# Attention and a GELU layer in one kernel: the last chunk's output stores joined to one per block, and two sums of chunk 2 moved behind the group sums

## The chip, the cores and the metric

The kernel runs on one core of a Trainium2 chip. The core has five engines that work side by side: TensorE (PE in the profile; its weight loads are PEld), VectorE (DVE), ScalarE (ACT), GpSimd (POOL) and SyncE (SP), which issues DMA transfers and computes nothing. ScalarE can issue transfers as well. Sixteen DMA engines move the data between the chip's memory and the core. The metric is the device time of one execution in microseconds (us).

## What is computed

Eight batches, eight heads, 576 positions, 64 columns per head. Linear attention, then a dense layer, an exact GELU and a second dense layer:

```python
q_s = softmax(q, axis=-1)          # per position
k_s = softmax(k, axis=2)           # over the positions
kv  = einsum('bhsd,bhse->bhde', k_s, v)
att = einsum('bhsd,bhde->bhse', q_s, kv)
x   = att.transpose(0, 2, 1, 3).reshape(4608, 512)
h   = x @ w_in                      # 512 x 2048
out = gelu(h) @ w_out               # 2048 x 512, 4608 rows of float32
```

(The two softmax lines stand for the reference's max, exp, sum and division.)

## The kernel before

**Chunks.** The 4608 rows of the output are 8 batches of 576 positions. Chunks 0 to 7 take the first 512 positions of one batch each (M = 512). The 64 positions that each batch has left (R = 64) are collected from all eight batches into a ninth chunk of 512 rows, chunk 8, which comes last. Inside chunk 8, block column j of half `half` holds two batches, 2 * (2 * half + j) and the one after it: partitions 0 to 63 belong to the first, 64 to 127 to the second.

**The order** in which each engine works is written out by hand: every engine and every queue runs its instructions in the order in which the code issues them, and waits on semaphores where it needs what another has made.

**Products with seven factors.** For chunks 2 to 8 the first dense layer is done by a scheme with 7 half-size products in place of 8 (`h_waves`), and so is the second layer of chunks 1 to 8 (`y_phase`, and `y_last` for chunk 8). Sums and differences of operands and of partial results, made on VectorE, take the place of the eighth product.

`h_waves` takes its output in four groups q = 0 to 3, in two waves: groups 0 and 1, then 2 and 3. `mm(m, q, ...)` issues product m for the groups named. Products accumulate in banks of the accumulator memory, kept in `held`: "A" (written by products 1, 6, 7, 4; in the profile qa), "B" (5 and 3; qb) and "C" (a copy of A, then product 2; qc). `seed(q)` copies A to C, `p5_copy(q)` copies B aside to `r`, `e_sum(q)` adds A to B (DVE qb L428), `r_sum(q)` adds A to `r` (DVE r L428). Product 7 writes into A again and so can't begin for a group before that group's `e_sum` has read A; product 4 can't before `r_sum`. `gelu(kind, ...)` on ScalarE takes a finished bank into `g`. `h_waves` is called with `mid` only for chunk 2; then the wave order is a little different, and the seeds of groups 2 and 3 are copied on VectorE.

`s_parts(c, p0, n, which)` makes the sums of `g` that the second layer needs, on VectorE: 0 makes `s5` (L393), 3 and 4 make the two halves of `s12` (L402), 2 two differences in place (L404, L405). `s12` is read by products 1 and 2 of the second layer, `s5` by product 5. In every chunk from 2 on, the add number 3 for rows 0 to 3 stands in `h_waves` ahead of `mm(6, 2, 3)` and the two group sums `e_sum(2)`, `e_sum(3)`; number 4 stands right behind those.

**The last chunk's output.** `y_last` computes chunk 8's rows in 128x256 blocks: two block columns j, and for each two halves of rows (`ysb[0]`, `ysb[1]`) and two halves of columns (c0 = 0 or 256), eight blocks in all. Each block's sum ends on VectorE (L428) or, for three of them, ScalarE (L769, L774). Then `store` sends the block out, with one transfer for each of the two batches: 64 partitions, 64 rows of 256 floats. Fourteen of these sixteen transfers are issued by SyncE; of the last two blocks one transfer each is issued by ScalarE (`both`). The tensor `dst` is `out` seen as [u, s, j, n]: batch parity, position, batch pair, column.

A transfer issued by SyncE or ScalarE carries one of eight semaphores in turn, and waits for the transfer that had the same one before it. The program ends when every transfer has landed.

The stores of the other chunks (`y_store`, L635) move 512 KB each: 128 partitions, one row of 4 KB each.

Of the kernel before, what the change touches and what calls it, by code (L numbers as in the profile page):

```python
# [16 lines left out]
def kernel(  # L17
# [16 lines left out]
    nc = tc.nc  # L34
    B, H, S, D = q.shape
# [3 lines left out]
    M = 128 * J  # L39
    R = S - M  # L40
# [25 lines left out]
    def bank(i, name="ps", shape=(128, 512)):  # L66
        return psum.tile(list(shape), FP32, tag=f"k{i}", name=name)
# [21 lines left out]
    HN = DM // 2  # L89
# [282 lines left out]
    def h_begin(c):  # L372
        st[c]["g"] = moe_sb.tile([128, NDF, M], BF16, tag="g", name="g", bufs=1)
# [53 lines left out]
    def tt(out, in0, in1, op=ALU.add, eng=nc.vector):  # L427
        eng.tensor_tensor(out=out, in0=in0, in1=in1, op=op)  # L428
# [33 lines left out]
    def h_waves(c, mid):  # L462

        h_begin(c)
        g, xT = st[c]["g"], st[c]["xT"]
        t1, t2, t3, t4 = (quad["t"][:, i] for i in range(4))
        mov = {1: xT[:, 0:2, 0:HT], 2: xT[:, 2:4, 0:HT], 3: xT[:, 2:4, HT:M], 4: t4, 5: t1, 6: t2, 7: t3}
        plain_w = {1: (0, 0), 2: (2, 0), 4: (2, HK)}  # L470
        sum_w = {3: 3, 5: 0, 6: 1, 7: 2}
        lo, hi = slice(0, HT), slice(HT, M)
        bank_of = {
            "A": ("bb", "x0", "x3", "ba"), "B": ("kv0", "kv1", "x1", "x2"), "C": ("x1", "x2", "kv0", "kv1"),
        }
        held = {}

        def take(kind, q):
            held[kind, q] = bank(roles[bank_of[kind][q]], "q" + kind.lower(), (128, 2, HT))

        def mm(m, *qs):
            for q in qs:
                kind = {5: "B", 3: "B", 2: "C"}.get(m, "A")
                if m in (1, 5):
                    take(kind, q)
                for u in range(2):
                    for k in range(2):
                        if m in plain_w:
                            k0, t0 = plain_w[m]
                            t = 2 * q + t0 + u  # L490
                            w = wi_bf[:, k0 + k, t * 128:(t + 1) * 128]
                        else:
                            t = 2 * (q % 2) + u
                            w = quad["s"][q // 2][:, sum_w[m], k, t * 128:(t + 1) * 128]
                        nc.tensor.matmul(  # L495
                            held[kind, q][:, u], w, mov[m][:, k],
                            start=(m in (1, 5) and u == 0 and k == 0), stop=(k == 1),
                            skip_group_check=True,
                        )

        def seed(q, eng=nc.scalar.copy):
            take("C", q)
            eng(out=held["C", q], in_=held["A", q])  # L503

        def p5_copy(q, eng):
            held["r", q] = quad["r"][:, q]
            eng(out=held["r", q], in_=held["B", q])

        def e_sum(q):
            tt(held["B", q], held["A", q], held["r", q])  # L510

        def r_sum(q):
            tt(held["r", q], held["A", q], held["r", q])

        def gelu(kind, *qs):
            up, half = {"C": (1, lo), "B": (1, hi), "A": (0, lo), "r": (0, hi)}[kind]
            for q in qs:
                t = 2 * q + (0 if up else HK)
                nc.scalar.activation(out=g[:, t:t + 2, half], in_=held[kind, q], func=AF.Gelu)  # L519

        vcopy, scopy = nc.vector.tensor_copy, nc.scalar.copy
        mm(1, 0, 1)
        seed(0)
        if mid:
            seed(1)
            mm(1, 2, 3)
            mm(2, 0, 1)
            gelu("C", 0, 1)
            mm(5, 0, 1)
        else:  # L530
            mm(5, 0, 1)
            seed(1)
        p5_copy(0, scopy)
        p5_copy(1, scopy)
        mm(6, 0, 1)
        x_sums(c, (3, 4) if mid else (3,))
        e_sum(0)
        e_sum(1)
        if not mid:
            x_sums(c, (4,))  # L540
        if mid:
            mid()
            mm(5, 2, 3)
            p5_copy(2, scopy)
            p5_copy(3, scopy)
        else:
            mm(2, 0, 1)
            gelu("C", 0, 1)
        mm(7, 0, 1)
        r_sum(0)  # L550
        r_sum(1)
        mm(3, 0, 1)
        if not mid:
            for q in (2, 3):
                mm(5, q)
                mm(1, q)
        mm(4, 0, 1)
        if mid:
            gelu("B", 0)
            seed(2, vcopy)  # L560
            gelu("B", 1)
            seed(3, vcopy)
            gelu("r", 0, 1)
        else:
            gelu("r", 0)
            gelu("B", 0, 1)
            gelu("r", 1)
            seed(2)
            seed(3)
        gelu("A", 0, 1)  # L570
        if not mid:
            p5_copy(2, vcopy)
            p5_copy(3, vcopy)
        s_parts(c, 0, 4, (3,))
        mm(6, 2, 3)
        e_sum(2)
        e_sum(3)
        s_parts(c, 0, 4, (4,))
        mm(2, 2, 3)
        gelu("C", 2, 3)  # L580
        mm(7, 2, 3)
        r_sum(2)
        r_sum(3)
        gelu("r", 2, 3)
        mm(3, 2, 3)
        mm(4, 2, 3)
        gelu("A", 2, 3)
        gelu("B", 2, 3)
        s_parts(c, 0, 4, (0,))
        s_parts(c, 0, 4, (2,))  # L590
        s_parts(c, 4, 4, (0,))
        s_parts(c, 4, 4, (3,))
        s_parts(c, 4, 4, (4,))
        turn_roles()
# [125 lines left out]
    def y_last(c):  # L720

        act, wgt = y_operands(c)
        names = (("x0", "yd"), ("x2", "yx"), ("x1", "ye"), ("ba", "ya"), ("bb", "yb"),
                 ("x3", "yd"), ("kv0", "ye"), ("kv1", "yb"))
        bd, bx, be, ba, bb, bd1, be1, bb1 = (bank(roles[r], n) for r, n in names)
        banks = [(bd, be, bb, ba), (bd1, be1, bb1, None)]
        ysb = [moe_sb.tile([128, 2, DM], FP32, tag="y_sb", name="y_sb", bufs=2) for i in range(2)]
        dst = out.rearrange("(j u s) n -> u s j n", j=J, u=2)  # L730

        def store(half, j, c0, engs):
            for u, eng in enumerate(engs):
                eng.dma_start(
                    out=dst[u, M:S, 2 * half + j, c0:c0 + HN],
                    in_=ysb[half][u * R:(u + 1) * R, j, c0:c0 + HN],
                )

        halves = [[(bank(roles["x2"], "ya") if ps is None else ps)[:, 0:HN] for ps in banks[j]] for j in range(2)]

        def mm(j, m, ps, first):
            for k in range(HK):
                nc.tensor.matmul(  # L743
                    ps, act[m][:, k, j * 128:(j + 1) * 128], wgt[m][:, k, :],
                    start=(first and k == 0), stop=(k == HK - 1), skip_group_check=True,
                )

        def parts(j):
            f = zeros32[:, j * HN:(j + 1) * HN]
            return (f, ysb[0][:, j, 0:HN], ysb[0][:, j, HN:DM], ysb[1][:, j, 0:HN], ysb[1][:, j, HN:DM])  # L750

        one = (nc.sync, nc.sync)
        both = (nc.scalar, nc.sync)
        for j in range(2):
            bd, be, bb, ba = halves[j]
            f, c11, c12, c21, c22 = parts(j)
            mm(j, 4, bd, True)
            nc.scalar.copy(out=f, in_=bd)
            if j == 0:
                mm(j, 3, bx[:, 0:HN], True)  # L760
                nc.scalar.copy(out=c12, in_=bx[:, 0:HN])
            mm(j, 5, be, True)
            tt(f, f, be, ALU.subtract)
            mm(j, 1, ba, True)
            tt(c22, f, ba)
            if j == 0:
                tt(c12, c12, be)
            mm(j, 2, bd, False)
            nc.scalar.copy(out=c21, in_=bd)  # L769
            store(1, j, 0, one)  # L770
            tt(c22, c22, c21, ALU.subtract)
            if j:
                mm(j, 3, be, False)
                nc.scalar.copy(out=c12, in_=be)  # L774
            store(0, j, HN, one)
            tt(c22, c22, c12)
        for j in range(2):
            bd, be, bb, ba = halves[j]
            f, c11, c12, c21, c22 = parts(j)
            mm(j, 6, bb, True)  # L780
            tt(c22, c22, bb)
            store(1, j, HN, both if j else one)
            mm(j, 7, ba, False)
            tt(c11, f, ba)
            store(0, j, 0, both if j else one)

    wi_cols = [256, 256, 512, 512, 512]
    wi_parts = [1, 1, 4, 2, 2]
# [337 lines left out]
```

## Time and profile before

| | |
|---|---|
| median of 3 runs | 259.1 us (258.95 to 259.1) |
| profiled execution | 259.09 us, of which span 257.3 us (first to last instruction) |
| TensorE clock granted over the span | 0.994 |
| TensorE, VectorE, ScalarE, GpSimd busy | 248.6, 208.2, 188.9, 67.6 us |
| sum of the last block done | 252.17 us |
| last store issued | 254.34 us |

In a profile line such as `L428 DVE TENSOR_TENSOR y_sb<-zeros,ya 128x256 f32` the line of the code comes first, then engine, operation, the tile written and those read, and the shape; `x14` counts the instructions of a group. In a timeline the first two numbers are start and length in us; in the chain of waits each line is a piece of the chain of work that ended last. `ACTq` and `SPq` are the sequencers that issue transfers. In the table by windows each engine shows its busy time; the last columns are the granted clock, the mean busy share of the 16 DMA engines and the GB/s that they moved. A DMA queue's line shows packets, MB and its share of the 16 engines' time. A line of DMA issues shows how many, their size and the median time from issue to landing.

The page's view of the span in 40 slices shows where each engine and the DMAs are busy; TensorE is full until the last two slices:

```profile
PE   7899999999999999999999999999999999999991
...
DMA  7999999993449905980598059805910420040024
```

### The profile page before, as it was taken

Reading aid. Unit: us, or ns where it says so; the run is one execution under the profiler, and the core shown is the slowest. Engines: PE = TensorE matmul, PEld = TensorE weight load, DVE = VectorE, ACT = ScalarE, POOL = GpSimd, SP = SyncE. Lnnn points to the kernel's source line nnn. Section 1 sums busy time; section 2 is a strip of 40 time slices with the busy share of each in tenths; the row PEclk is TensorE's granted clock in tenths of the full one; section 3 lists DMA queues with packets and bytes.
Section 4 is the critical chain, followed back from the end, with each engine's and each line's share of the span. In section 5 each row is a group of like instructions: output and inputs, shape, how many; then the busy total and the mean of one; then the engine's idle time right before and its main releaser. Section 6 shows DMA issues by size and latency. Waiting matters only on the chain.

```text
span 257.3 us, 6512 instructions
## 1 busy us (share of the span) xinstructions
PE 248.6 (97%) x2670; PEld 195.1 (76%) x2670; DVE 208.2 (81%) x364; ACT 188.9 (73%) x320; POOL 67.6 (26%) x65
## 2 busy tenths in 40 slices
PE   7899999999999999999999999999999999999991
PEld 3444444448887888888888888888888888888880
DVE  1878796998978979896989798979897989398951
ACT  4876887799978895899589958995896686068610
POOL 1530024001645067006700670067002700040000
PEclk9999999999999999999999999999999999999997
DMA  7999999993449905980598059805910420040024
GB/s 240 399 384 425 402 405 400 397 414 133 84 153 346 263 17 143 315 326 1 137 305 338 3 131 333 316 0 132 250 33 0 130 117 3 0 160 8 1 64 102
DMA packets 43166, 50.23 MB, mean 195 GB/s; under 512 B 20224, under 2 KB 30464, under 8 KB 42880
## 3 DMA queue, kind: packets, MB, share of 16 engines
q1 hardware_dynamic: 42736, 49.39, 56.9%
q10 hardware_dynamic: 400, 0.43, 0.7%
q8 instruction: 21, 0.34, 0.5%
q14 instruction: 9, 0.07, 0.1%
HBM read 36.70 MB, written 9.44 MB: 179 GB/s over the span
## 4 chain that ended last, share of the span: by engine, by line
PE 91%; DMA 4%; DVE 1%; ACT 1%; issue 0%; ACTq 0%; POOL 0%; DVEq 0%
PE qa L495 18%; PE ps L377 11%; PE ya L673 10%; PE yd L673 10%; PE qb L495 9%; PE ye L673 5%; PE ps L616 5%; PE yb L673 5%; PE qc L495 4%; PE yx L673 4%; PE kv L225 2%; DMA f<-in_v_dram 2%; DMA touch<-in_moe_w_in_dram 2%; PE ps L343 2%; PE ya L743 1%; PE yd L743 1%
## 5 line engine op out<-in xcount | busy, mean ns | idle before, releaser
L495 PEld LDWEIGHTS <-quad_s 128*128 128x128 bf16 x448 | 43.8, 98 | 6.1 <-issue 1.0
L673 PEld LDWEIGHTS <-g 128*128 128x128 bf16 x448 | 43.3, 98 | 5.8 <-issue 0.4
L269 POOL TENSOR_TENSOR e<-e,recq 128x2048 bf16<-128x2048 bf16 (+1 forms) x9 | 27.4, 3047 | 73.4 <-DVE recq L264 40.5
L495 PEld LDWEIGHTS <-wi_bf 128*128 128x128 bf16 x336 | 32.8, 98 | 4.0
L673 PEld LDWEIGHTS <-s 128*128 128x128 bf16 x336 | 32.9, 98 | 3.8
L495 PE MATMUL qa<-quad_t,quad_s 128*128 128x256 bf16 x224 | 29.5, 272 | 0.2
L377 PE MATMUL ps<-xT,wi_bf 128*128 128x512 bf16 x128 | 28.3, 379 | 0.0
L428 POOL TENSOR_TENSOR y_sb<-y_sb 128x512 f32<-128x512 f32 x14 | 19.4, 1389 | 24.2 <-DVE y_sb L428 21.3
L263 DVE TENSOR_REDUCE qsum<-e 128x16 f32<-128x1024 bf16 (+1 forms) x12 | 20.9, 1746 | 4.9 <-ACT e L173 4.8
L377 PEld LDWEIGHTS <-wi_bf 128*128 128x128 bf16 x128 | 12.2, 98 | 15.4 <-DVE wi_bf L814 0.9
L503 ACT COPY qc<-qa 128x512 f32<-128x512 f32 x26 | 13.9, 577 | 12.0 <-PE qa L495 11.5
L519 ACT ACTIVATE g<-r 128x512 bf16<-128x512 f32 x28 | 17.3, 630 | 7.3 <-DVE r L428 7.3
L428 DVE TENSOR_TENSOR qb<-qa,r 128x512 f32<-128x512 f32 x28 | 18.1, 693 | 5.5 <-ACT g L519 3.1
L383 ACT ACTIVATE g<-ps 128x512 bf16<-128x512 f32 x32 | 17.8, 600 | 6.1 <-PE ps L377 5.8
L173 ACT ACTIVATE e<-f 128x512 bf16<-128x512 f32 (+1 forms) x42 | 20.5, 556 | 2.1 <-DMA f<-in_q_dram 2.1
L519 ACT ACTIVATE g<-qc 128x512 bf16<-128x512 f32 x28 | 15.2, 594 | 7.1 <-PE qc L495 7.1
L402 DVE TENSOR_TENSOR s<-g 128x1024 bf16<-128x1024 bf16 x28 | 18.5, 682 | 0.2 <-ACT g L519 0.2
L190 POOL CAST v_aug<-f 128x576 bf16<-128x576 f32 x26 | 17.6, 709 | 4.2 <-DMA f<-in_v_dram 3.9
L428 DVE TENSOR_TENSOR r<-qa,r 128x512 f32<-128x512 f32 x28 | 18.0, 682 | 0.7 <-PE qa L495 0.4
L178 ACT ACTIVATE ek<-f 128x2304 bf16<-128x2304 f32 (+1 forms) x10 | 17.2, 1734 | 0.5 <-DMA f<-in_k_dram 0.5
L519 ACT ACTIVATE g<-qb 128x512 bf16<-128x512 f32 x28 | 15.1, 595 | 0.7 <-PE qb L495 0.7
L495 PE MATMUL qb<-quad_t,quad_s 128*128 128x256 bf16 x112 | 15.5, 273 | 0.0
(100 smaller groups left out, 466.8 us busy)
## 6 DMA issues: line engine op xcount, KB each, us to landing
out_dram<-y_sb SPq DMA_DIRECT2D x16, 512.0 KB, 3.4
f<-in_k_dram SPq DMA_DIRECT2D x6, 1152.0 KB, 9.6
f<-in_v_dram SPq DMA_DIRECT2D x6, 1152.0 KB, 11.6
f<-in_q_dram SPq DMA_DIRECT2D x6, 1024.0 KB, 7.9
w<-in_moe_w_in_dram SPq DMA_DIRECT2D x6, 512.0 KB, 9.3
f<-in_v_dram SPq DMA_DIRECT2D x8, 288.0 KB, 6.3
f<-in_q_dram SPq DMA_DIRECT2D x4, 512.0 KB, 9.0
w<-in_moe_w_out_dram SPq DMA_DIRECT2D x2, 1024.0 KB, 11.9
```

The costliest lines, as they stand in the source:

```text
L173: nc.scalar.activation(out=dst[:, i], in_=src[:, u], func=AF.Exp)
L178: nc.scalar.activation(out=ek[b % 2][:, i:i + n], in_=st[b]["kf"][:, i:i + n].rearrange("p x (n d) -> p x n d", n=NS), func=AF.Exp,)
L190: eng.tensor_copy(out=o, in_=i)
L263: nc.vector.reduce_sum(out=qsum, in_=st[b]["eq"][:, :, i * w:(i + 1) * w, :], axis=AX.X)
L269: eng.tensor_tensor(out=e, in0=e, in1=st[b]["recq"].unsqueeze(3).to_broadcast([128, J, w, D]), op=ALU.mult,)
L377: nc.tensor.matmul(ps, wi_bf[:, dm, t * 128:(t + 1) * 128], st[c]["xT"][:, dm, :], start=(dm == 0), stop=(dm == NDM - 1),)
L383: nc.scalar.activation(out=st[c]["g"][:, t, :], in_=ps, func=AF.Gelu)
L402: tt(out=s12[:, a, half], in0=g[:, a, half], in1=g[:, b, hi], op=ALU.add)
L428: eng.tensor_tensor(out=out, in0=in0, in1=in1, op=op)
L495: nc.tensor.matmul(held[kind, q][:, u], w, mov[m][:, k], start=(m in (1, 5) and u == 0 and k == 0), stop=(k == 1), skip_group_check=True,)
L519: nc.scalar.activation(out=g[:, t:t + 2, half], in_=held[kind, q], func=AF.Gelu)
L673: nc.tensor.matmul(ps[:, j * HN:(j + 1) * HN], act[m][:, k, j * 128:(j + 1) * 128], wgt[m][:, k, :], start=(first and k == 0 and j == 0), ...
```

## The change

Two edits.

1. In `y_last`, `store` issues one transfer per block instead of two. Its source is the block's 128 partitions, its target `dst[:, M:S, ...]`, with the two batches as the outermost dimension: 2 x 64 rows of 256 floats, the two batches being 576 rows of `out` apart. Eight transfers are left. Six are issued by SyncE; those of the two blocks `store(0, 1, HN)` and `store(0, 1, 0)` by ScalarE. None of the eight shares its semaphore with another of them any more.
2. In `h_waves` with `mid` (chunk 2 alone), the add number 3 of `s12` for rows 0 to 3 moves from ahead of `mm(6, 2, 3)` and the group sums to behind the group sums, where number 4 was; number 4 moves to behind `s5`'s first add. The other chunks keep their order. The instructions are the same ones.

```diff
@@ h_waves
-        s_parts(c, 0, 4, (3,))
+        if not mid:
+            s_parts(c, 0, 4, (3,))
         mm(6, 2, 3)
         e_sum(2)
         e_sum(3)
-        s_parts(c, 0, 4, (4,))
+        s_parts(c, 0, 4, (3,) if mid else (4,))
         mm(2, 2, 3)
...
         s_parts(c, 0, 4, (0,))
+        if mid:
+            s_parts(c, 0, 4, (4,))
         s_parts(c, 0, 4, (2,))
@@ y_last
-        def store(half, j, c0, engs):
-            for u, eng in enumerate(engs):
-                eng.dma_start(
-                    out=dst[u, M:S, 2 * half + j, c0:c0 + HN],
-                    in_=ysb[half][u * R:(u + 1) * R, j, c0:c0 + HN],
-                )
+        def store(half, j, c0, eng=nc.sync):
+            eng.dma_start(
+                out=dst[:, M:S, 2 * half + j, c0:c0 + HN],
+                in_=ysb[half][:, j, c0:c0 + HN],
+            )
...
-        one = (nc.sync, nc.sync)
-        both = (nc.scalar, nc.sync)
...
-            store(1, j, 0, one)
+            store(1, j, 0)
...
-            store(0, j, HN, one)
+            store(0, j, HN, nc.scalar if j else nc.sync)
...
-            store(1, j, HN, both if j else one)
+            store(1, j, HN)
...
-            store(0, j, 0, both if j else one)
+            store(0, j, 0, nc.scalar if j else nc.sync)
```

## The prediction

> **What bounds the kernel now.** I read the page first, then the timeline of the last 15 us, the DMA issues, the busy time by windows, and the chain of waits around chunk 2's second pair of groups.
>
> ```profile
> span 257.3 us, 6512 instructions
> ...
> PE 248.6 (97%) x2670; PEld 195.1 (76%) x2670; DVE 208.2 (81%) x364; ACT 188.9 (73%) x320; POOL 67.6 (26%) x65
> ...
> PE 91%; DMA 4%; DVE 1%; ACT 1%; issue 0%; ACTq 0%; POOL 0%; DVEq 0%
> ```
>
> TensorE is 91% of the chain: a change of order pays only where TensorE waits. After its last product the kernel has only stores left, and there the end is set by who issues and moves them:
>
> ```profile
> 251.33 1.37 ACTq L734 DMA_DIRECT2D out_dram<-y_sb  x2
> 251.75 0.42 DVE L428 TENSOR_TENSOR y_sb<-zeros,ya 128x256 f32<-128x256 f32 x1 [0.45 <-PE ya L743]
> ```
> ```profile
> 254.34 0.55 SPq L734 DMA_DIRECT2D out_dram<-y_sb  x1
> ```
>
> The last sum is done at 251.75 + 0.42 = 252.17. SyncE is still issuing: its last store goes out at 254.34, since 14 issues of 0.47 to 1.35 us each stand in one queue. That store lands 2.0 us later (next fence), at 256.34, and the span ends 0.96 later. So about 4.2 us lie between the last sum and the last landing, 2.2 of them SyncE's queue.
>
> ```profile
> out_dram<-y_sb SPq DMA_DIRECT2D x14, 64.0 KB, 2.0
> ...
> f<-in_k_dram ACTq DMA_DIRECT2D x1, 288.0 KB, 3.1
> ...
> out_dram<-y_sb ACTq DMA_DIRECT2D x2, 64.0 KB, 2.0
> touch<-in_v_dram ACTq DMA_DIRECT2D x1, 0.1 KB, 4.1
> ```
> ```profile
> q10 hardware_dynamic: 400, 0.43, 0.7%
> ```
>
> q10 is ScalarE's queue, and its packets can be counted out. It carries one load of 128 rows, three of 16 rows (touch, of v, w_in and w_out) and two stores of 64 rows: 128 + 48 + 128 = 304 rows, at one packet a row. The other 96 are 16 for each of the six transfers, one closing packet per DMA engine. So every transfer was cut into 16 pieces, even the one of 16 rows of 8 bytes: the cut goes by rows, not by bytes. In all of them the first dimension on both sides is 128, 64 or 16.
>
> **The stores.** Removed: 16 issues, each of 64 rows of 1 KB. Added: 8 issues, each of 128 rows of 1 KB, six on SyncE and two on ScalarE (the last two blocks of output columns that finish on it). The bytes stay at 1 MB, 1024 packets. What is new is the shape of the target: [2 batches][64 rows][256], against 128 partitions at the source. No profiled transfer has a first dimension below 16, so the number of engines that share such a transfer is unknown, and has to be bounded from both sides: 16, as in all rows above, or 2, one for each index of the first dimension. I take 2. The cut seen above goes by rows, and a target whose first dimension has two entries 576 rows apart can be cut along it only once; to get 16 pieces the cut would have to go through two dimensions together, which no transfer here shows.
>
> The Trainium skill says the same in "DMA: Bandwidth & Descriptors", "Why a DMA increments its semaphore by 16 and not by 1": the number of engines is the largest up to 16 that divides the slowest dimension, other than 1, of both sides. By that rule each new store uses 2 engines and the result is the forecast. Its section "Rules for kernel authors" also says the opposite of halves: one transfer of 128 partitions rather than two of disjoint halves; that advice alone would give rival A. No run here shows either yet.
>
> Pace of one engine on 1 KB packets, from two ends:
>
> ```profile
> core 0: us, PE busy (x) PEld busy (x) DVE busy (x) ACT busy (x) POOL busy (x), PEclk, DMA share, GB/s
> 3.50:5.50 2.00, 2.00 (x4) 0.77 (x3) 0.00 (x0) 1.09 (x3) 0.00 (x0) 1.00 1.08 378
> ...
> 229.20:231.00 1.80, 1.80 (x19) 1.62 (x17) 1.69 (x4) 1.22 (x4) 0.00 (x0) 1.00 0.99 403
> 252.00:254.00 2.00, 0.00 (x0) 0.00 (x0) 0.17 (x1) 0.00 (x0) 0.00 (x0) 1.00 0.67 162
> ```
>
> From 3.5 to 5.5 the first loads of q run, rows of 1 KB over 128 partitions: 378 / (1.08 x 16) = 21.9 GB/s for a busy engine, 46.8 ns a packet. From 252 to 254 the old stores run, over 64 partitions each: 162 / (0.67 x 16) = 15.1, or 67.8 ns. From 229.2 to 231 the stores of chunk 7 run, rows of 4 KB: 403 / (0.99 x 16) = 25.4, which for 1 KB would be 40.3 ns. So storing is not slower in itself; the 67.8 belongs to sixteen engines crowding on half the partitions. Two engines, one for each half, are nearer to the first window: I take 46.8 and keep 40.3 and 67.8 as ends. (The page named above gives about 27 GiB/s an engine; that would be 35 ns and, as an estimate, 266.4 us.)
>
> With two engines each store puts 64 packets on each, 64 x 46.8 ns = 3.0 us, and I take it that all eight use the same two (else it is rival C). The eight become ready within 7.9 us (first issue 244.28, last sum 252.17) but need 24 us of service, so from the second store on the two engines are never idle, and neither which queue issues a store nor how fast matters. The first issue moves to 243.85 (next part). Fixed cost of a store: 2.0 us less its four packets per engine of 68 ns, 1.73. Last landing: 243.85 + 1.73 + 512 x 0.0468 = 269.54, where it was 256.34. Nothing in the program is queued behind the stores but the closing waits, so no engine's work is held; the old cover, TensorE's products up to 251.7, hides only the first 7 us of it.
>
> **Chunk 2's s12.** VectorE's add of the first half of s12 (L402) stood before the two group sums. The chain there, and TensorE's products:
>
> ```profile
> 80.86 0.64 ACT g L519
> ...
> 81.52 0.69 DVE s L402
> 82.21 0.62 DVE qb L428
> ...
> 82.88 1.19 PE qa L495 x8
> ```
> ```profile
> 80.75 1.19 PE L495 MATMUL qa<-quad_t,quad_s 128*128 128x256 bf16 x8
> 81.78 1.04 PE L495 MATMUL qc<-xT,wi_bf 128*128 128x256 bf16 x8
> 82.88 1.19 PE L495 MATMUL qa<-quad_t,quad_s 128*128 128x256 bf16 x8
> ```
>
> Eight products follow each other in 0.87 us (first start to next group's first start, elsewhere in this chain). Group 82.88 could start at 81.78 + 0.87 = 82.65: 0.23 lost, and inside it 1.19 - 1.04 = 0.15 more while it waits for the second group sum. The last group of this wave takes 1.08 rather than 1.04, 0.04 more. Sum 0.42, say 0.43 with roundings. In the new order a group sum starts when its products are done. For the first pair of groups VectorE started 0.11 after the end of the fourth product (76.71 to 76.82). Here the fourth starts at 80.75 + 3 x 0.11 = 81.08 and takes 0.27 (the page's mean), so the first sum starts at 81.46; the second group's products start at 81.35, held by the seed as before, and its sum at 82.06; with 0.69 each they end at 82.15 and 82.75, ahead of 82.65 and 83.09 when TensorE wants the banks. The add of s12 itself now runs 82.66 to 83.35, when the first r sum's products are just done (83.37). So the stall goes and no new one comes. The other half of s12 (0.69) moves behind s5; VectorE has as many adds in that stretch as before, so those after it keep their times (the last of s12 ended at 88.82, the last in place at 90.15, for which GpSimd waits). The first reader of s12 is the product at 90.94, or 90.51 now: 1.7 us cover it. Without that cover up to 0.69 would come back; with it all 0.43 stay. No DMA is issued by what is moved, and nothing of SyncE's or GpSimd's queue is passed. The 0.15 inside the group at 80.75 is a wait for the seeds, which stays. After 82.88 the chain is TensorE to the end, so I pass 0.43 on to it.
>
> **The sum**, against the profiled execution: 259.09 us, of which the span is 257.30 and 1.79 lies around it; it is within 0.01 of the median, 259.1. New: 269.54 + 0.96 + 1.79 = 272.29, so +13.2 = -0.43 (chunk 2) + 13.6 (tail). With 40.3 ns it is 269.0, with 67.8 ns 283.0.
>
> **Rivals.**
> A. The cut still gives 16 engines (faster). The same formula gives the end 243.85 + 1.73 + (1024 / k) x 0.0468 for k engines, until the last issue decides. With 16, SyncE's queue of 14 is gone, the last store goes out on ScalarE at 251.77 and lands after 2.2 (2.0 and four more packets per engine): 253.97 + 0.96 + 1.79 = 256.7, 2.4 us less. For it: every transfer of the page was cut in 16, and the count of rows, 128, is a multiple of 16. Against: the cut never had to cross a dimension. It decides from k = 5 on: break-even with 256.34 is at 1024 x 0.0468 / 10.76 = 4.5 engines.
> B. Two engines, at the pace of the old stores' packets: 283.0. For it: the same rows of out, in the same direction. Against: the crowding goes with sixteen engines.
> C. Four engines at work at a time, by a finer cut or because one store's two engines are not the next one's: 243.85 + 1.73 + 256 x 0.0468 = 257.56, and 260.3 in all. Nothing in the page speaks for it but that the source has 128 rows to cut.
> D. The s12 move alone counts, if the stores came out even: 258.7. By the formula that needs k between 4 and 5, and no k that divides 128 lies there, so I give it 0.01.
>
> **Numbers.** Forecast 0.74; B 0.13; A 0.09; C 0.03; D 0.01. The likeliest gives 272.3, its own range 268 to 277; to leave out no more than 2 in 10 I reach over B: 267 to 284. A stays outside. What a measurement of this kernel can tell from no change is about 0.2%, 0.5 us: faster 0.09 (A), within 0.01 (D), slower 0.90 (the rest).
>
> **What would show it.** Two engines: after 252 us the DMA share is near 2/16 and the rate near 44 GB/s until about 269; the stores' landing grows from one to the next to more than 15 us; every compute engine is idle for the last 17 us. The q10 count: 128 + 48 + 256 rows, 64 closing packets of the four loads and 2 x 2 of the stores = 500; with 16 engines it would be 528. B shows as 30 GB/s. In chunk 2: no L402 in the chain between 80 and 83, and the group after the qc products starts about 0.23 earlier. Landings of 2 to 2.5 us and a span near 255 would make the forecast wrong at its first step, the number of engines; a right DMA share with another end would make only the pace wrong.

## The result and the profile after

| | before | after |
|---|---|---|
| median | 259.02 us (6 runs) | 271.28 us (6 runs, 270.74 to 271.39) |
| profiled execution, its span | 259.09, 257.3 us | 270.93, 269.1 us |
| last sum on VectorE done | 252.17 us | 251.58 us |

The time is 1.0477 times that of before (95% interval 1.0458 to 1.0495): 12.3 us slower. The work on the engines ended 0.6 us earlier (0.17 us of that was gained before chunk 2's reordered sums, and not by the edit). Everything lost lies behind it.

The page of the changed kernel, its 40 slices (of 6.7 us each now):

```profile
PE   7999999999999999999999999999999999999300
...
DMA  7999999990499439904970695087007000300111
GB/s 241 400 398 426 402 402 401 398 370 5 78 304 373 69 67 287 390 7 117 316 312 3 181 333 231 0 235 162 0 2 234 2 0 18 143 1 26 46 48 38
```

The last two slices have no products in them at all (in the kernel before, only the last slice was not full), and through the last three the DMAs are busy for a tenth and move 38 to 48 GB/s: a slow trickle, not a burst. Busy time by windows, last two columns DMA share and GB/s:

```profile
252.00:267.00 15.00, 0.00 (x0) 0.00 (x0) 0.00 (x0) 0.00 (x0) 0.00 (x0) 0.65 0.14 48
255.00:267.00 12.00, 0.00 (x0) 0.00 (x0) 0.00 (x0) 0.00 (x0) 0.00 (x0) 0.56 0.14 48
267.00:268.30 1.30, 0.00 (x0) 0.00 (x0) 0.00 (x0) 0.00 (x0) 0.00 (x0) 0.50 0.07 24
```

0.14 of 16 engines is 2.2: two engines that are never idle. What is above 2 is overlap: in the trace's records a packet takes 46 ns, and the next one on the same engine begins about 42 ns after it began. 48 GB/s is 24 for each. In the last window the rate halves, since the transfers end within it. The queue's packets and the issues of the stores say the same:

```profile
q10 hardware_dynamic: 500, 0.56, 0.7%
```
```profile
out_dram<-y_sb SPq DMA_DIRECT2D x6, 128.0 KB
...
out_dram<-y_sb ACTq DMA_DIRECT2D x2, 128.0 KB
```

500 is the count forecast for two engines: 128 + 48 + 256 rows, 64 closing packets of the four loads, and 2 for each of the two stores; 16 engines would leave 528. The profile's lines give no landing times here, but the trace keeps each raising of a semaphore. Each of the eight stores has its semaphore raised by two engines only, and they land between 248.7 and 268.0 us, the slowest 15.5 us after its issue.

What SyncE waited for in the last 29 us (total in us, how often, the longest):

```profile
SPq L1121 <- DMA out_dram<-y_sb: 9.4, 2, 6.7
SPq L736 <- DVE y_sb L428: 3.5, 3, 2.0
```

Before, its closing waits for stores came to 1.3 us.

In chunk 2 the chain of waits has lost its sums:

```profile
79.83 0.71 DVE qc L503
80.54 0.04 issue
80.58 1.19 PE qa L495 x8
81.78 0.87 PE qc L495 x8
82.65 0.87 PE qa L495 x8
83.52 0.87 PE qb L495 x8
84.40 0.87 PE qa L495 x8
```

From 81.78 on TensorE runs each group in 0.87 us with no wait between. The seeds before it (qc, 1.19) still cost what they did.

### The profile page after: what moved, and what is told of

Its sections match the earlier page's. It is cut to its first block, busy times and chain, and to the rows that moved or that the text cites. A ratio compares the mean times of both kernels' runs of the same rounds, so it can differ in the third digit from the quotient of the medians.

```text
span 269.1 us, 6495 instructions
## 1 busy us (share of the span) xinstructions
PE 248.5 (92%) x2664; PEld 195.9 (73%) x2670; DVE 208.4 (77%) x364; ACT 188.8 (70%) x320; POOL 67.7 (25%) x65
## 4 chain that ended last, share of the span: by engine, by line
PE 88%; DMA 4%; DVE 1%; POOL 0%; issue 0%; ACT 0%; SPq 0%
PE qa L495 18%; PE ps L377 10%; PE ya L676 9%; PE yd L676 9%; PE qb L495 9%; PE ye L676 5%; PE ps L619 5%; PE yb L676 5%; PE qc L495 5%; PE yx L676 4%; DMA f<-in_v_dram 2%; PE kv L225 2%; PE ps L343 2%; DMA f<-in_q_dram 2%; PE ya L745 1%; PE yd L745 1%
## 5 line engine op out<-in xcount | busy, mean ns | idle before, releaser
L676 PEld LDWEIGHTS <-g 128*128 128x128 bf16 x448 | 43.3, 98 | 5.8 <-issue 0.4
L377 PEld LDWEIGHTS <-wi_bf 128*128 128x128 bf16 x128 | 12.3, 98 | 15.2 <-issue 0.5
L495 PE MATMUL qb<-quad_t,quad_s 128*128 128x256 bf16 x112 | 15.5, 273 | 0.0
```

Of the source, the lines that this page charges most:

```text
L377: nc.tensor.matmul(ps, wi_bf[:, dm, t * 128:(t + 1) * 128], st[c]["xT"][:, dm, :], start=(dm == 0), stop=(dm == NDM - 1),)
L495: nc.tensor.matmul(held[kind, q][:, u], w, mov[m][:, k], start=(m in (1, 5) and u == 0 and k == 0), stop=(k == 1), skip_group_check=True,)
L676: nc.tensor.matmul(ps[:, j * HN:(j + 1) * HN], act[m][:, k, j * 128:(j + 1) * 128], wgt[m][:, k, :], start=(first and k == 0 and j == 0), ...
```

## Experiments

Twelve microseconds could come from two engines, or from something else in a 128-row store to two batches. The first four kernels separate the two edits and these two causes; each was timed in several rounds beside the kernel before, whose median in these rounds was 259.18 us.

**e1: the s12 move alone.** `h_waves` of the changed kernel, `store` of the one before.

> Chunk 2's reordered s12 alone, the stores as before. If the two waits of TensorE at the group sums (0.43 us in the trace before) go through to the end: 258.6 us against 259.0, and no step over 0.12 us between the products from 81.7 to 85.3. Rival: the 0.43 us are taken up by a later wait, and the time is 259.0.

258.83 us, ratio 0.9985 (0.9976 to 0.9993): 0.35 us faster, between 0.2 and 0.6. The chain of waits has the same form as above:

```profile
81.02 1.19 PE qa L495 x8
82.21 0.87 PE qc L495 x8
83.08 0.88 PE qa L495 x8
```

So the 0.43 us goes through to the end, in size within what can be measured.

**e2: the joined stores alone.** `h_waves` as before.

> The joined stores alone, s12 as before. If the two parts add up: 271.7 us, 0.4 more than the changed kernel, with the same 500 packets on ScalarE's queue. Rival: the stores hold something besides the tail, and the time differs from 271.7 by more than 0.5 us.

271.46 us, ratio 1.0475 (1.0461 to 1.0488), 500 packets. The stores alone make the loss; nothing else is held up. The stall of chunk 2 is back in its chain, of the kind that the kernel before had:

```profile
81.28 0.69 DVE s L402
81.97 0.62 DVE qb L428
82.59 0.04 issue
82.64 0.60 PE qa L495 x4
```

**e3: two queues.** The s12 move, and the old stores with one of each pair on ScalarE:

```diff
-            store(1, j, 0, one)
+            store(1, j, 0, both)
-            store(0, j, HN, one)
+            store(0, j, HN, both)
-            store(1, j, HN, both if j else one)
+            store(1, j, HN, both)
-            store(0, j, 0, both if j else one)
+            store(0, j, 0, both)
```

> s12 as in the change; two stores of 64 rows per block as before, but one on ScalarE and one on SyncE for all eight blocks. If SyncE's row of 14 issues set the end before: the last two go out at about 251.7, land 2.0 to 2.2 later, 256.6 us in all. Rival: the DMA engines, not the issuing, set the end before, and the time stays at 258.6 (the s12 move alone).

256.89 us, ratio 0.9917 (0.9901 to 0.9933). SyncE's last issue, which was at 254.34, is now at 251.84:

```profile
251.84 0.47 SPq L737 DMA_DIRECT2D out_dram<-y_sb  x1
```

So before, the row of 14 issues did set the end, as the prediction read it; and that row can be shortened without joining any store.

**e4: rows interleaved.** Eight joined stores on the same queues as in the change, but chunk 8's partitions take the two batches in turn, so that the 64 positions can be the first dimension:

```diff
-                out=f[(b % 2) * R:(b % 2 + 1) * R, b // 2, :, :],
+                out=f[b % 2:128:2, b // 2, :, :],
...
-                            ps[c, bb * R:(bb + 1) * R], kvc_of(bb, hp)[pr],
-                            st[b]["qT"][pr, bb // 2, hp, bb % 2 * R:(bb % 2 + 1) * R],
+                            ps[c, bb // 2 * 128 + bb % 2:bb // 2 * 128 + 128:2], kvc_of(bb, hp)[pr],
+                            st[b]["qT"][pr, bb // 2, hp, bb % 2:128:2],
...
-        dst = out.rearrange("(j u s) n -> u s j n", j=J, u=2)
+        dst = out.rearrange("(j u s) n -> s u j n", j=J, u=2)
...
-                out=dst[:, M:S, 2 * half + j, c0:c0 + HN],
+                out=dst[M:S, :, 2 * half + j, c0:c0 + HN],
```

> s12 and the number and queues of the stores as in the change, but chunk 8's partitions take the two batches in turn (2 x position + batch), so the same 128 rows of each store go out with the 64 positions as first dimension and the two batches inside. Theory, the cut goes along the first dimension: 16 engines, 528 packets on ScalarE's queue, landing 2.2 us after the last issue at 251.7, 256.7 us. Rival, a store of 128 rows to two batches is slow whatever the order of its dimensions (far-apart rows, length of one issue): 271 us again.

256.83 us, ratio 0.991 (0.9897 to 0.9923). The rows, their places in `out`, the sizes and the queues are those of the change; only the order of the two dimensions differs, and with it the partition on which each row lies; the time is 14.5 us less. Its queue line and issues:

```profile
q10 hardware_dynamic: 528, 0.56, 0.8%
```
```profile
out_dram<-y_sb SPq DMA_DIRECT2D x6, 128.0 KB, 2.1
...
out_dram<-y_sb ACTq DMA_DIRECT2D x2, 128.0 KB, 2.1
```

528 packets, sixteen engines, and 2.1 us to landing for the same 128 KB. The rival (far-apart rows, or the length of one issue) falls. e3 and e4 both beat both kernels; between themselves they can't be told apart.

The next four put one part of e3 back at a time. The kernel before had a median of 259.03 us in these rounds.

**e5: the last block alone joined.**

```diff
-            store(0, j, 0, both)
+            if j:
+                nc.scalar.dma_start(out=dst[:, M:S, j, 0:HN], in_=ysb[0][:, j, 0:HN])
+            else:
+                store(0, j, 0, both)
```

> As e3_two_queues (256.9), but the last block alone goes out as one store of 2 x 64 rows, on ScalarE. Two engines carry 64 packets each, 64 x 42.4 ns = 2.7 us, in place of four per engine: 258.8 to 259.3, and 930 packets on ScalarE's queue (240 + 7 x 80 + 128 + 2). Rival, only the pile of eight such stores costs, one of them is as quick as another store: 256.9.

259.30 us, ratio 1.0007 (0.9995 to 1.0019), 930 packets. One such store in the last place costs 2.4 us against e3 (2.3 by the two ratios, as e3 was timed in other rounds). By the pace of the changed kernel, 42.7 ns a packet, 60 packets more for each of two engines are 2.6.

**e6: 62 rows and 2.** The last block's two stores cut in two, all with one dimension of rows:

```diff
+        def last(cuts):
+            j = 1
+            for lo, hi in cuts:
+                for u, eng in enumerate(both):
+                    eng.dma_start(
+                        out=dst[u, M + lo:M + hi, j, 0:HN],
+                        in_=ysb[0][u * R + lo:u * R + hi, j, 0:HN],
+                    )
...
-            store(0, j, 0, both)
+            if j:
+                last(((0, 62), (62, 64)))
+            else:
+                store(0, j, 0, both)
```

> As e3_two_queues, but each of the last block's two stores of 64 rows is cut into one of 62 rows and one of 2, so no target has two dimensions. Theory of the divisor (as many engines, up to 16, as divide the first dimension): 62 rows and 2 rows use 2 engines each, 64 packets on each of the two as in e5, 258.8 to 259.5, and 868 packets on ScalarE's queue (240 + 7 x 80 + 62 + 2 + 2 + 2). Rival, it is the outer dimension of two batches that does it, and 62 rows spread over 16 engines or nearly: 257.4 as in e7, and at least 890 packets.

**e7: 60 rows and 4.** The same with `last(((0, 60), (60, 64)))`.

> The control to e6: 60 rows and 4. By the divisor 15 engines and 4: 257.4, for the one issue more on each queue (0.5 us), and 883 packets on ScalarE's queue (240 + 7 x 80 + 60 + 15 + 4 + 4). Rival, cutting a store in two is itself what costs in e6: the same time as e6.

e6: 259.21 us, ratio 1.0008 (0.9999 to 1.0017). e7: 256.38 us, ratio 0.9895 (0.988 to 0.9909). Two rows more in a store cost 2.8 us. The packets of ScalarE's queue, first e6, then e7:

```profile
q10 hardware_dynamic: 868, 0.82, 1.3%
```
```profile
q10 hardware_dynamic: 883, 0.82, 1.2%
```

Both counts are those of the divisor rule to the packet: 2 closing packets for 62 rows and 2 for 2, 15 for 60 rows and 4 for 4. So it isn't the second dimension as such: the first dimension's size decides, through the largest number up to 16 that divides it. e7's time was expected at 257.4 and is 1.0 better: the small stores of 4 rows were issued in 0.26 and 0.28 us, not 0.55, so they add little. It is even 0.5 below e3, though the two intervals overlap a little. In the two profiled runs 0.22 of that lies ahead of the stores (the last sum is done at 251.59 us in e7, at 251.81 in e3); the rest stays open.

**e8: the first two blocks joined.** Stores that go out early, on SyncE, the others as in e3:

```diff
         def store(half, j, c0, engs):
+            if (half, j, c0) in ((1, 0, 0), (0, 0, HN)):
+                nc.sync.dma_start(
+                    out=dst[:, M:S, 2 * half + j, c0:c0 + HN], in_=ysb[half][:, j, c0:c0 + HN])
+                return
             for u, eng in enumerate(engs):
```

> As e3_two_queues, but the first two blocks go out as one store of 2 x 64 rows each, on SyncE. Two engines need 2 x 2.7 = 5.4 us for them, from about 245.2 to 250.7, while TensorE still computes until 251.3: hidden, 256.9. Rival, the later stores queue behind them on these two engines and on SyncE: 257.5 or more.

257.82 us, ratio 0.9951 (0.9935 to 0.9968): 0.9 us slower than e3, and the expectation of a hidden transfer falls. Its waits of SyncE at the end, then its stores' landings beside those of e3:

```profile
SPq L741 <- DMA out_dram<-y_sb: 1.8, 1, 1.8
```
```profile
out_dram<-y_sb SPq DMA_DIRECT2D x6, 64.0 KB, 3.3
out_dram<-y_sb ACTq DMA_DIRECT2D x6, 64.0 KB, 3.5
```
```profile
out_dram<-y_sb SPq DMA_DIRECT2D x8, 64.0 KB, 2.0
out_dram<-y_sb ACTq DMA_DIRECT2D x8, 64.0 KB, 2.3
```

Two things delay the small stores, and the trace's semaphore events show both. They have a sixteenth of their rows on each of the two occupied engines: of the first one on ScalarE, issued at 247.45 us, fourteen engines' shares had landed by 250.77 and the last two at 252.01 and 252.05. (Even the fourteen are late: in e3 fifteen shares of the same store had landed by 249.63. Why the free engines got their shares later stays open.) And a store waits for the one that had its semaphore before: SyncE stood still for 1.8 us until the second joined store landed, at 251.69. It is this wait that reaches the end. SyncE's last store goes out 1.1 us later than in e3 (251.84), and then lands after 2.1 us, against 1.9 in e3:

```profile
252.95 0.57 SPq L741 DMA_DIRECT2D out_dram<-y_sb  x1
```

## Why the prediction was right

- **The number of engines: right.** It was the step that decided, and it had to be chosen without a row that shows it. Of the prediction's reasons, the cut along the first dimension holds; the 576 rows between the two batches play no part, since e4 has them too and uses sixteen engines. 500 packets, two busy engines, and e4, which swaps the two dimensions (and the partitions with them), show it. e6 and e7 show the rule behind it. The Trainium skill states that rule ("DMA: Bandwidth & Descriptors", "Why a DMA increments its semaphore by 16 and not by 1"), and here the traces agree with it for 2 x 64, 62, 60, 4 and 2 rows.
- **The same two engines for all eight: right.** The rate stays at 48 GB/s with several stores outstanding; rival C (four at work) would show twice that.
- **The pace: right in kind, 10% off in size.** Taken: 46.8 ns a packet, from the loads. Measured: 48 GB/s over two engines, 42.7 ns, so 512 x 4.1 ns = 2.1 us less. This is the term that was mis-sized, and its own row shows why: the 378 GB/s of the loads were divided by a share of 1.08, which is above 1 only because packets overlap. Sixteen full engines make 378 / 16 = 23.6 GB/s each, 43.3 ns. The forecast of 272.3 us was 1.4 too high against the profiled 270.93: 2.1 for the pace and 0.16 for the first issue, which came earlier than forecast, less about 0.9 where the two engines moved under 48 GB/s (31 from 244.9 to 247, 37 from 252 to 253). Why they were slower there stays open, so it is partly luck that the end came out closer than the pace. Rival B (67.8 ns) was rightly set aside: two engines never showed that pace. e3, with stores of 64 partitions, and e4, with stores of 128, show the two paces side by side in the windows of their tails:

```profile
251.00:253.00 2.00, 0.35 (x4) 0.07 (x1) 0.42 (x1) 0.00 (x0) 0.00 (x0) 1.00 0.80 198
```
```profile
252.00:253.50 1.50, 0.00 (x0) 0.00 (x0) 0.00 (x0) 0.00 (x0) 0.00 (x0) 1.00 0.50 169
```

  198 / (0.80 x 16) = 15.5 GB/s for a busy engine in e3, 169 / (0.50 x 16) = 21.1 in e4: 66 and 48 ns a packet. By the trace's records the 1 KB packets themselves take longer, 69 ns in the median in e3 and 46 in e4; the closing packets take 9 ns in both, so their greater number in e3 isn't the reason. What makes a packet of a 64-partition store longer was not tried. The advice of the Trainium skill on the same page, "DMA: Bandwidth & Descriptors" ("Rules for kernel authors"), to use one transfer of 128 partitions instead of two halves was worth nothing measurable between these two kernels, which end within 0.1 us of each other; followed with the two batches as first dimension, as in the change, it cost 12 us.
- **Rival A's arithmetic: right, for another kernel.** With sixteen engines it gave 256.7; e4, where they are had, measured 256.83. The expected gain of the change was real, and its price was the shape of one access pattern.
- **The s12 move: right.** -0.43 forecast, -0.35 (-0.2 to -0.6) measured alone. The chain agrees: the second layer's first products start here before and after, 0.59 us apart, and 0.17 of that was there when the pair began (80.75 and 80.58 us), which leaves 0.42.

```profile
85.86 1.75 PE yd L673 x16
```
```profile
85.27 1.75 PE yd L676 x16
```

- **What lies behind the stores: right for this change.** It said that neither the queue nor the order of the issues would matter. The steady 48 GB/s fits that, but no run put the joined stores on other queues. e2 adds up with e1 to within 0.2 us, so nothing but the tail was held. But the remark that the cover of TensorE's products hides the first 7 us was too kind as a general rule: e8 shows that a slow store under that cover delays the quick ones behind it.

## What to carry to other kernels

Look at the first dimension of both sides of a transfer before joining transfers: here 128 and 64 gave sixteen engines, while 62, 60, 4 and 2 gave as many as the largest divisor up to 16. Price the packets on that many engines. If two outer dimensions can trade places, put one first whose size is a multiple of 16, and lay out the tile for it. The number of closing packets in the queue's line (its packets less the rows) tells how many engines were used, without any timing. And take the pace of a full engine from bytes over elapsed time, not from a busy share above 1.

## What was not expected

- An issue can take long while the engines that it goes to are backed up. In the changed kernel SyncE's last two stores took 3.67 and 5.01 us to issue, against 0.5 to 0.7 for the first four:

```profile
253.62 5.01 SPq L736 DMA_DIRECT2D out_dram<-y_sb  x1
```

  Four and five stores had not yet landed when these two began. It cost nothing here, for the two engines went on at 48 GB/s. That the backlog makes the issue long is a reading of these rows; what depth of the queue brings it on was not tried.
- The granted clock of TensorE falls once it has no work: 0.56 over 255 to 267 us and 0.50 at the end, in the windows above. With no products left nothing waits for it, but the mean of the span falls with it, to 0.976.
